# Soft-MoE attention on one core: five instead of four half batches of output stored between the last weight loads

## The chip, the core and the metric

The kernel runs on one core of a Trainium2 chip. The metric is the device time of one execution in microseconds (us). Data goes between device memory and the on-chip buffers by DMAs, which the queue of SyncE (SP) issues one after another and 16 DMA engines carry out. TensorE (PE) multiplies, VectorE (DVE) and ScalarE (ACT) copy and do elementwise work.

## The reference

An attention with a sigmoid in place of the softmax gives x, 3584 tokens by 768. A soft mixture of experts then mixes the tokens into 32 slots, sends each group of four slots through its own expert (two matrices), and mixes the slots back into tokens. Cut to what matters:

```python
scores = scale * np.matmul(q, k.transpose(0, 1, 3, 2)) - np.log(S)   # 8 batches, 12 heads, 448 tokens, 64
attn_out = np.matmul(1.0 / (1.0 + np.exp(-scores)), v)
x = attn_out.transpose(0, 2, 1, 3).reshape(B * S, H * D)             # 3584 x 768
logits = x @ phi                                                     # 32 slots, 4 for each of 8 experts
slot_input = softmax(logits, axis=0).T @ x
for e in range(E):                                                   # w1: 8 x 768 x 1024, w2: 8 x 1024 x 768
    slot_out[e] = np.maximum(slot_input[e] @ w1[e], 0.0) @ w2[e]
out = softmax(logits, axis=1) @ slot_out                             # 3584 x 768, float32
```

## The kernel before

The attention runs first, batch by batch, and takes some 280 us. What follows is the part that the change touches. The expert weights come in 128 units of 128 x 768 numbers (384 KB each): 64 of w1, then 32 of w2 for the first 384 output columns (`hf` 0), then 32 of w2 for the last 384 (`hf` 1). Each unit takes the next tile of a ring of 68 (`ring_tile`, `wa0` to `wa46` and `wb0` to `wb20`; L77). The first 68 units are loaded during and right after the attention. Of the rest, `load_more` (L509) puts one load behind a piece of work that has freed a tile, up to a limit of 128 - `N_LATE`: in the kernel before, units 0 to 111 are in SP's queue that way, and the last 16 are left over. I call these the late units; they are numbers 112 to 127.

The first product with w2 gives `st`, the slot outputs for columns 0 to 383. With it the first half of the output can be computed, while the second product with w2 still runs. That is the loop at L613, of 16 steps. Step i multiplies units 96 + 2i and 97 + 2i (`w2_step`, L588). In steps 3 to 10 it also computes the first column half of one batch's output, batch i - 3 (`out_batch`): eight matmul instructions (L565), an ACT copy of 128 rows and a DVE copy of 96 rows (L570) into two tiles of the same ring, and four stores that are put on a list. A half batch is 448 rows of 384 numbers: two stores of 192 KB and two of 144 KB, 672 KB together, each by its own DMA (L579).

Where those stores and the late loads stand in SP's queue is written out by hand: in the first `N_MIX` of these steps, `store(4)` issues the four stores of the half batch, and then `N_LATE // N_MIX` late units are loaded. The other half batches stay on the list until all loads are issued (L626). So SP's queue is, before: unit 111, four stores, four units, four stores, four units, four stores, four units, four stores, units 124 to 127, and then 16 stores in a row. Steps 10 to 13 have a few multiplications that compute nothing (`warm`, L583).

After the last `w2_step` comes a chain: ACT copies the sum (`gather`, L594), PE adds the groups (L599), DVE copies the result to `st` (L601), PE computes the second half of batch 0's output (L565), ACT and DVE copy it (L570), and SP stores it (L579). Then follow batches 1 to 7 in the same way, 32 stores in all.

SP takes its instructions in order, and each DMA also waits for one of eight completion counters that are used in turn: it can't be issued before the eighth DMA ahead of it has landed.

Of the kernel before, what the change touches and what calls it, by code (L numbers as in the profile page):

```python
# [26 lines left out]
UNIT = 768  # L27
N_A = 47
N_B = 21
N_LATE = 16  # L30
N_MIX = 4
NATT = 5
QW = 2 * S
NP = B * NPR
# [13 lines left out]
def soft_moe_attention(ctx: ExitStack, tc: tile.TileContext, qk, v, phi, w1, w2, cst, out):  # L48
# [36 lines left out]
    def load_unit():  # L85
        n = state["next"]
        if n >= len(units):
            return
        state["next"] = n + 1
        u = units[n]  # L90
        t = ring_tile()[:]
        nc.sync.dma_start(t, w1[u[1:]] if u[0] == "w1" else w2[u[1:]])
        utile[u] = t
# [415 lines left out]
    def load_more():  # L509
        if state["next"] < len(units) - N_LATE:  # L510
            load_unit()
# [49 lines left out]
    def out_batch(hf, b, st):  # L561
        pf = [px_tile() for _ in range(2)]
        for j in range(4):
            r = slice(32 * j, 32 * j + 32)
            nc.tensor.matmul(  # L565
                pf[j // 2][0:TOK[j], j % 2, 0:HALF], lt_all[r, b, 0:TOK[j]], st[r, :], start=True, stop=True)
        for g in range(2):
            n = TOK[2 * g]
            ov = ring_tile()[0:n, :].rearrange("p (j c) -> p j c", j=2)
            (nc.scalar.copy if g == 0 else nc.vector.tensor_copy)(ov, pf[g][0:n, :, 0:HALF])  # L570
            r0 = b * S + TOF[2 * g]
            for j in range(2):
                stores.append((out[r0 + j * n:r0 + j * n + n, hf * HALF:(hf + 1) * HALF], ov[:, j, :]))
# [3 lines left out]
    def store(n):  # L577
        for _ in range(min(n, len(stores))):
            nc.sync.dma_start(*stores.popleft())  # L579
# [33 lines left out]
    for i in range(2 * E):  # L613
# [3 lines left out]
        if 3 <= i < 3 + B:  # L617
            out_batch(0, i - 3, st)
            if i < 3 + N_MIX:
                store(4)  # L620
                for _ in range(N_LATE // N_MIX):
                    load_unit()
# [43 lines left out]
```

## Time and profile before

| | |
|---|---|
| time, median of 3 runs | 391.66 us (391.07 to 392.79) |
| profiled execution, its time | 390.38 us |
| its span, from the first to the last instruction | 388.6 us |
| PE busy | 365.3 us (94% of the span) |
| DVE busy | 226.1 us (58%) |
| ACT busy | 187.5 us (48%) |
| DMA, mean over the span | 251 GB/s |

The profiled execution took 390.38 us, 1.8 us more than its span. All stretches and durations below are of this one execution. PE's busy share is an average over stages: the attention is PE's, while the end of the program, from about 290 us, has to be read by itself, since there the DMA engines are always busy. Times of single instructions count from the start of the span. A DMA has three times that matter: when SP issues it, how long the issuing instruction holds SP, and how long after the issue the data has landed.

### The profile page before, as it was taken

To read this page: it belongs to the slowest core of one execution; us is meant where nothing else is said; L and a number is where in the kernel's file an instruction comes from. 1 tells how busy PE (TensorE), PEld (TensorE's weight loads), DVE (VectorE), ACT (ScalarE), POOL (GpSimd) and SP (SyncE) were. 2 spreads that over 40 slices of the span, in tenths; PEclk is the share of its full clock that TensorE was granted. 3 is DMA by queue.
4 is the path that set the end of the run, shared out by engine and by line. 5 is a ranking of instruction groups with operands and counts; after the bars stand their busy time and mean duration, and the time that the engine had idled before them with its cause. 6 is when DMAs were issued, how large, how long until landed. Compare 5 with 4: busy or idle time off the path is not lost.

```text
span 388.6 us, 9551 instructions
## 1 busy us (share of the span) xinstructions
PE 365.3 (94%) x3994; PEld 189.8 (49%) x3994; DVE 226.1 (58%) x518; ACT 187.5 (48%) x243; POOL 3.3 (1%) x13
## 2 busy tenths in 40 slices
PE   8999999999999999999999999999989989978760
PEld 7444556554555654555554455554455543224220
DVE  3655677775887677697767777776543410430250
ACT  5655676564567556566635666564531110320240
POOL 1000000000000000000000000000020000000000
PEclk9999999999999999999999999999999999999995
DMA  7766855662784567476446654323999999999997
GB/s 228 260 240 236 300 171 183 237 252 83 265 295 138 178 229 255 135 257 240 177 140 228 238 164 156 143 101 98 292 406 400 400 400 400 398 407 399 373 302 231
DMA packets 42363, 97.52 MB, mean 251 GB/s; under 512 B 4816, under 2 KB 16720, under 8 KB 42320
## 3 DMA queue, kind: packets, MB, share of 16 engines
q1 hardware_dynamic: 42320, 96.91, 70.3%
q8 instruction: 31, 0.51, 0.5%
q14 instruction: 12, 0.10, 0.1%
HBM read 85.43 MB, written 11.47 MB: 249 GB/s over the span
## 4 chain that ended last, share of the span: by engine, by line
PE 80%; DMA 14%; DVE 1%; SPq 1%; ACT 1%; issue 0%; ACTq 0%
PE b L189 29%; PE b L171 24%; DMA wa<-in_w_dram 8%; PE b L182 6%; DMA wb<-in_w_dram 6%; PE b L198 5%; PE b L312 4%; PE px L522 4%; PE b L218 3%; PE b L407 1%; PE px L565 1%; PE px L539 1%; SPq L579 1%; DMA out_dram<-wa 1%; DVE wa L570 0%
## 5 line engine op out<-in xcount | busy, mean ns | idle before, releaser
L161 ACT ACTIVATE att<-b,nbias 128x896 f32<-128x896 f32 x144 | 131.9, 1015 | 12.0 <-PE b L171 12.0
L189 PE MATMUL b<-att,v 128*64 128x448 f32 x576 | 115.3, 545 | 0.0
L171 PE MATMUL b<-qs,ks 64*128 64x448 f32 x864 | 95.9, 372 | 0.0
L171 PEld LDWEIGHTS b<-qs,ks 64*128 64x128 f32 x864 | 77.4, 184 | 26.6 <-PE b L182 11.3
L189 PEld LDWEIGHTS b<-att,v 128*64 128x64 f32 x576 | 38.5, 136 | 61.6 <-issue 50.2
L161 ACT ACTIVATE attm<-b,nbias 128x896 f32<-128x896 f32 x24 | 24.2, 1008 | 70.4 <-PE b L182 70.4
L207 DVE COPY xT<-b 128x896 f32<-128x896 f32 x23 | 25.1, 1092 | 32.7 <-PE b L198 32.7
L152 DVE TENSOR_TENSOR qs<-qkt,qs 128x448 fp32r<-128x448 f32 x48 | 30.0, 625 | 1.7
L152 DVE TENSOR_TENSOR ks<-qkt,ks 128x384 fp32r<-128x384 f32 x48 | 26.8, 558 | 1.6
L213 DVE STREAM_TRANSPOSE y<-xT 128x448 f32<-128x448 f32 x48 | 27.3, 617 | 0.4
L182 PE MATMUL b<-qkt 64*64 64x448 f32 x192 | 24.1, 570 | 0.0
L150 DVE CAST qs<-qkt 128x448 fp32r<-128x448 f32 x48 | 18.2, 380 | 8.8 <-DMA qkt<-in_qk_dram 7.7
L198 PE MATMUL b<-attm,v 64*64 64x448 f32 x192 | 22.4, 537 | 0.0
L570 DVE COPY wa<-px 96x768 f32<-96x768 f32 x13 | 12.2, 952 | 13.7 <-PE px L565 12.9
L570 ACT COPY wa<-px 128x768 f32<-128x768 f32 x13 | 10.3, 799 | 18.1 <-PE px L565 14.2
L565 PE MATMUL px<-st,lt_all 32*128 32x384 f32 (+1 forms) x128 | 16.7, 524 | 1.5 <-DVE st L601 0.7
L312 PE MATMUL b<-y,dr 32*32 32x192 f32 x896 | 17.7, 331 | 0.2 <-ACT dr L303 0.2
L218 PEld LDWEIGHTS b<-xT,phit 128*32 128x32 f32 x384 | 9.1, 109 | 17.0 <-issue 13.4
L522 PE MATMUL px<-wa,sT 128*32 128x256 f32 x282 | 16.8, 381 | 0.6 <-DVE sT L380 0.6
L150 DVE CAST ks<-qkt 128x384 fp32r<-128x384 f32 x47 | 16.6, 353 | 0.0
L218 PE MATMUL b<-xT,phit 128*32 128x96 f32 (+1 forms) x384 | 16.0, 266 | 0.2
L601 DVE COPY st<-px 128x384 f32<-128x384 f32 x2 | 1.1, 557 | 25.3 <-PE px L599 25.3
(132 smaller groups left out, 229.3 us busy)
## 6 DMA issues: line engine op xcount, KB each, us to landing
wa<-in_w_dram SPq DMA_DIRECT2D x92, 384.0 KB, 7.7
qkt<-in_qk_dram SPq DMA_DIRECT2D x48, 448.0 KB, 3.8
wb<-in_w_dram SPq DMA_DIRECT2D x36, 384.0 KB, 5.7
v<-in_v_dram SPq DMA_DIRECT2D x24, 448.0 KB, 5.7
out_dram<-wa SPq DMA_DIRECT2D x26, 192.0 KB, 3.3
out_dram<-wa SPq DMA_DIRECT2D x26, 144.0 KB, 3.3
dr<-zd SPq DMA_DIRECT2D x28, 64.0 KB, 2.0
out_dram<-wb SPq DMA_DIRECT2D x6, 192.0 KB, 5.5
```

The lines of the kernel that those rows point to most:

```text
L150: copy(dst[:, 0, :], src)
L152: nc.vector.tensor_tensor(out=dst[:, 1, :], in0=src, in1=dst[:, 0, :].bitcast(F32), op=ALU.subtract)
L161: nc.scalar.activation(att[:], sc[:, :, 0:S], AF.Sigmoid, bias=nbias, scale=QSCALE)
L171: nc.tensor.matmul(sc[:, h, 0:S], ks[r, z, c * P:(c + 1) * P], qs[r, y, :], start=(z + y == 0), stop=(z == 1))
L182: nc.tensor.matmul(sc[r, h, 0:S], t[d, S + NQK:QW], t[d, 0:S], start=True, stop=True)
L189: nc.tensor.matmul(avs["p", p][r, 0:S], vs[n][:, i * (NFULL + 1) + c, r], atts[p, c][:, h, :], start=(start and c == 0), stop=(stop and c ...
L198: nc.tensor.matmul(avs["p", 2 * n + i][d, 0:S], vt[r, NFULL, d], att[r, h, :], start=start, stop=stop)
L207: nc.vector.tensor_copy(xTs[n][:], avs[n][:, :, 0:S])
L213: nc.vector.transpose(ys[b][:, hp, :], xTs["p", p])
L218: nc.tensor.matmul(lp[32 * j:32 * j + 32, 0:TOK[j]], phi_sb[:, p % NPR, :], xTs["p", p][:, TOF[j]:TOF[j] + TOK[j]], start=(first and m == ...
L312: nc.tensor.matmul(sl[a // 2][32 * j:32 * j + 32, a % 2, 0:NPR * BLK], drs[b][32 * a:32 * a + 32, j, c * BLK:(c + 1) * BLK], y[32 * a:32 * ...
L522: nc.tensor.matmul(ph[32 * j:32 * j + 32, uu, 0:256], sT[:, 3 * kh + kc, :], utile[("w1", e, 2 * uu + j // 2, kh)][:, kc * 256:(kc + 1) * ...
```

## The change

Two constants change. `N_LATE` goes from 16 to 15, so unit 112 is loaded by `load_more`, ahead of the first stores. `N_MIX` goes from 4 to 5, so five half batches are stored among the late loads, each followed by 15 // 5 = 3 units instead of four. Nothing is added or removed: there are as many loads, stores, copies and matmuls as before, of the same sizes.

```diff
-N_LATE = 16
-N_MIX = 4
+N_LATE = 15
+N_MIX = 5
```

In SP's queue, at the first half batch that is stored (`wa_4226` and `wa_4228` are its two output tiles before, `wa_4228` and `wa_4230` now; `wa_4234` before and `wa_4029` now hold unit 112; - is before, + is now; "x2" is two instructions in a row):

```order
 L92 DMA wa_4019<-in_w_dram 128x768
-L579 DMA out_dram<-wa_4226 128x384 x2
-L579 DMA out_dram<-wa_4228 96x384 x2
-L92 DMA wa_4234<-in_w_dram 128x768
+L92 DMA wa_4029<-in_w_dram 128x768
+L579 DMA out_dram<-wa_4228 128x384 x2
+L579 DMA out_dram<-wa_4230 96x384 x2
 L92 DMA wb_4236<-in_w_dram 128x768
```

Unit 112 moved ahead of the four stores of batch 0's first half; unit 113 keeps its place.

In SP's queue, at the last loads, before (`wb_4312` to `wb_4318` are units 124 to 127, the stores behind them those of batches 4 and 5):

```order
L92 DMA wb_4312<-in_w_dram 128x768
L92 DMA wb_4314<-in_w_dram 128x768
L92 DMA wb_4316<-in_w_dram 128x768
L92 DMA wb_4318<-in_w_dram 128x768
L579 DMA out_dram<-wa_4330 128x384 x2
L579 DMA out_dram<-wa_4332 96x384 x2
L579 DMA out_dram<-wa_4344 128x384 x2
L579 DMA out_dram<-wa_4346 96x384 x2
```

and now (units 122 to 124, the stores of batch 4, units 125 to 127, the first stores of batch 5):

```order
L92 DMA wb_4308<-in_w_dram 128x768
L92 DMA wb_4310<-in_w_dram 128x768
L92 DMA wb_4312<-in_w_dram 128x768
L579 DMA out_dram<-wb_4324 128x384 x2
L579 DMA out_dram<-wb_4326 96x384 x2
L92 DMA wb_4332<-in_w_dram 128x768
L92 DMA wa_4334<-in_w_dram 128x768
L92 DMA wa_4336<-in_w_dram 128x768
L579 DMA out_dram<-wa_4348 128x384 x2
```

The four stores of batch 4's first half moved from behind unit 127 to ahead of unit 125. Twelve stores are left behind the last load, where 16 were.

On PE, at the last two steps of the second product with w2 (units 124 to 127; the order of PE's instructions is the same, only the tiles that the units lie in differ):

```order
 L583 MATMUL po<-csb 128x128 x3
 L588 MATMUL po<-wb_4312,h_3681 32x384 x2
-L588 MATMUL po<-wb_4314,h_3681 32x384 x2
-L588 MATMUL po<-wb_4316,h_3681 32x384 x2
-L588 MATMUL po<-wb_4318,h_3681 32x384 x2
+L588 MATMUL po<-wb_4332,h_3681 32x384 x2
+L588 MATMUL po<-wa_4334,h_3681 32x384 x2
+L588 MATMUL po<-wa_4336,h_3681 32x384 x2
```

Three of these four units now stand behind the fifth half batch's stores in the queue, where all four stood together.

## Rows read from the trace of the kernel before

**Rows 1.** The page's second part, the span in 40 equal slices of 9.7 us: the mean busy share of the DMA engines in tenths, and what they moved.

```profile
DMA  7766855662784567476446654323999999999997
GB/s 228 260 240 236 300 171 183 237 252 83 265 295 138 178 229 255 135 257 240 177 140 228 238 164 156 143 101 98 292 406 400 400 400 400 398 407 399 373 302 231
```

**Rows 2.** The chain of work that ended last, in order of time, from 339.67 us: start, duration, what it was. A DMA's duration here is from its issue to its landing.

```profile
339.67 5.40 DMA wb<-in_w_dram
...
345.13 5.40 DMA wb<-in_w_dram
...
350.60 5.46 DMA wb<-in_w_dram
...
356.12 6.00 DMA wb<-in_w_dram
...
362.17 0.86 PE po L588 x4
...
363.11 0.49 ACT tmp L594
...
363.64 0.93 PE px L599 x2
...
364.59 0.57 DVE st L601
...
365.20 0.94 PE px L565 x6
...
366.16 0.81 ACT wa L570
...
366.99 0.54 SPq L579
```

**Rows 3.** Busy time of the engines in two stretches, from the first store to the first store of the second column half, and from there to 387.5 us. The last three columns are PE's granted clock, the DMA engines' busy share and GB/s.

```profile
334.00:366.97 32.97, 27.04 (x188) 9.09 (x182) 8.57 (x10) 7.25 (x11) 0.00 (x0) 1.00 1.04 398
366.97:387.50 20.53, 7.78 (x52) 3.04 (x52) 6.70 (x8) 5.48 (x7) 0.00 (x0) 0.76 0.88 288
```

**Rows 4.** SP's queue in order of time: start, time until the last of the group had been issued, line, what, how many. Groups of four unit loads and of four stores between the first late loads and the last.

```profile
342.26 3.20 SPq L92 DMA_DIRECT2D wb<-in_w_dram  x4
345.64 1.91 SPq L579 DMA_DIRECT2D out_dram<-wb  x4
347.76 3.16 SPq L92 DMA_DIRECT2D wb<-in_w_dram  x4
351.21 1.88 SPq L579 DMA_DIRECT2D out_dram<-wb  x4
353.27 3.17 SPq L92 DMA_DIRECT2D wb<-in_w_dram  x4
```

**Rows 5.** The same view, three unit loads in a row ahead of the first store, and the first store.

```profile
329.92 0.33 SPq L92 DMA_DIRECT2D wa<-in_w_dram  x1
330.89 0.33 SPq L92 DMA_DIRECT2D wa<-in_w_dram  x1
331.87 0.33 SPq L92 DMA_DIRECT2D wa<-in_w_dram  x1
334.40 0.34 SPq L579 DMA_DIRECT2D out_dram<-wa  x1
```

**Rows 6.** ACT in order of time: the copies of batch 4's and batch 7's first half (idle time before them in brackets, with what ended it).

```profile
341.38 0.80 ACT L570 COPY wa<-px 128x768 f32<-128x768 f32 x1 [1.11 <-PE px L565]
...
350.42 0.80 ACT L570 COPY wa<-px 128x768 f32<-128x768 f32 x1 [2.78 <-DMA out_dram<-wb]
```

**Rows 7.** The stores' line in the stretch 362.5 to 366.5 us, after the last load has landed: how many, duration of the issuing instruction (least, median, most, ns), first and last start; and from issue to landing. Then the first and the last of these eight issues in SP's order of time.

```profile
L579 SPq DMA_DIRECT2D out_dram<-wa x8: 351/425/450, 362.7 to 366.1; - x8
...
DMA to landing us min/median/max: 3.1/3.3/3.6
...
362.68 0.35 SPq L579 DMA_DIRECT2D out_dram<-wa  x1
...
366.07 0.44 SPq L579 DMA_DIRECT2D out_dram<-wa  x1
```

**Rows 8.** The same line from 366.9 to 385 us, the 32 stores of the second column half, with the last issue.

```profile
L579 SPq DMA_DIRECT2D out_dram<-wa x32: 350/442/727, 367.0 to 384.2; - x32
...
DMA to landing us min/median/max: 2.8/3.3/3.7
...
384.25 0.50 SPq L579 DMA_DIRECT2D out_dram<-wa  x1
```

**Rows 9.** What SP waited for from 366.9 us to the end (us in total, times, longest); L662 is the end of the program.

```profile
SPq L662 <- DMA out_dram<-wa: 2.8, 2, 2.4
SPq L579 <- ACT wa L570: 0.6, 2, 0.4
SPq L662 <- PEq L662: 0.6, 2, 0.4
SPq L579 <- DVE wa L570: 0.2, 1, 0.2
```

**Rows 10.** PE in order of time, at the last steps of the second product with w2 and in the output of the second half (idle time before the group in brackets).

```profile
359.26 2.75 PE L588 MATMUL po<-wb,h 128*32 128x384 f32 x12 [1.46 <-DMA wb<-in_w_dram]
362.17 0.84 PE L588 MATMUL po<-wb,h 128*32 128x384 f32 x4 [0.16 <-DMA wb<-in_w_dram]
...
368.96 3.56 PE L565 MATMUL px<-st,lt_all 32*128 32x384 f32 x24 [0.35 <-DVE wa L570]
372.71 2.70 PE L565 MATMUL px<-st,lt_all 32*128 32x384 f32 x16 [0.19 <-DVE wa L570]
```

**Rows 11.** Stretches after PE's last matmul; the third number from the right is the granted clock.

```profile
376.50:377.00 0.50, 0.00 (x0) 0.00 (x0) 0.00 (x0) 0.00 (x0) 0.00 (x0) 1.00 1.00 313
...
378.00:379.00 1.00, 0.00 (x0) 0.00 (x0) 0.00 (x0) 0.00 (x0) 0.00 (x0) 0.50 0.95 298
```

## The prediction

> **What bounds the kernel now.** I read the slices first. In the last quarter of the span the DMA engines' share is 9 in every slice, at about 400 GB/s, and in the last three slices it stays high while the rate falls to 302 and 231 [rows 1]. So the end belongs to DMA in some form, and the question is which form where. The chain answers that [rows 2]. Up to 362.12 us it is a row of unit loads, each issued when an earlier one has landed: PE waits for weights, weights wait for their place in a full queue. The last load is issued at 356.12 and lands 6.00 us later. Then comes a chain that moves almost nothing: the last four matmuls (0.86), `gather` (0.49), the sum over groups (0.93), the copy to `st` (0.57), batch 0's second half on PE (0.94), its ACT copy (0.81), and at 366.99 the first store of the second half. From there on 32 stores are left.
>
> Two stretches, then. Up to 366.97 the engines move 398 GB/s at a share of 1.04; behind it 288 GB/s at 0.88 [rows 3]. In the second stretch, who is the limit? SP issues 32 stores between 366.99 and 384.25, so one every 17.26 / 31 = 0.557 us; the issuing instruction alone holds it for 0.442 (median), and a store lands 3.3 us after its issue, as it did at 363 to 366 us [rows 2, 7, 8]. SP waits for a copy for only 0.6 + 0.2 us in all of that, and for no earlier store's landing [rows 9]. If the engines were the limit and SP ran ahead, eight DMAs would be under way and a landing would take 8 x 0.557 = 4.5 us. It takes 3.3, with no growth. I therefore read the last stretch as SP's: it starts when the first second-half copy is ready, and its length is 32 issues plus one landing.
>
> **The change part by part.** *The batch that moves ahead of the last load.* Up to the last load the DMA engines are full, so what is put in front of it delays it. Unit 112 only changes places with a group of stores and stays ahead of the last load in both; the one thing that crosses is four stores, 672 KB. Its cost there, three ways:
>
> - From the cycle: groups of four loads start at 342.26, 347.76 and 353.27, so a cycle of four loads and four stores is 5.50 us [rows 4]. Loads alone go one per (331.87 - 329.92) / 2 = 0.975 us [rows 5]. The stores' part is 5.50 - 3.90 = 1.60.
> - From the bytes: 672 KB are 0.688 MB, at 398 GB/s [rows 3] 1.73 us.
> - From stores with no loads beside them: eight issues from 362.68 to 366.07, so 0.484 us each [rows 7], four are 1.94.
>
> I take 1.7, nearest to the first two, since those rows are of the mixed stretch into which the batch goes; the ends are 1.6 and 1.94.
>
> *Does SP wait for the moved batch's copies, with three loads behind it?* The copies of batch 4's first half start at 341.38 and take 0.80 (ACT) [rows 6]. Now its stores come to their turn after three cycles of 5.50 and three of three loads each; counted from the first store at 334.40 [rows 5], four cycles of 3 x 0.975 + 1.7 = 4.6 give about 353. That wait costs nothing, and there are 11 us of cover.
>
> *The twelve stores left behind the last load.* Before, SP finished issuing the sixteenth at 366.07 + 0.44 = 366.51 and stood until the copy was ready at 366.97 [rows 2, 7]. So these stores already fit into the time of the chain, with 0.46 us to spare. Four fewer of them give SP a longer pause, 4 x 0.484 = 1.9 us more, in which nothing else is ready. This is where the expected gain would have to be, and it is spent on waiting: the work that was taken out had cover, and the place it was put into has none.
>
> *The chain from the last landing to the first second-half store* keeps its instructions, 366.99 - 362.12 = 4.87 us, and begins 1.7 later. PE's last steps meet their units one by one as before; the longest wait there is 1.46 us [rows 10]. Units 125 to 127 come 1.7 later than before, 124 at the same time, so the added wait falls between 124 and 125 and does not stack on the old one in full.
>
> *The last 32 stores.* Same number, same issuing engine. Bounds: 0 if the pace stays 0.557; up to 4 x (0.557 - 0.484) = 0.3 us more, if the first few went at the quicker pace of the stretch before, which now has ended earlier [rows 7, 8]. I take 0.
>
> Sum: 390.38 + 1.7 = 392.1 for the profiled execution. It lies 1.28 below the median of the runs shown, so on the median 391.66 + 1.7 = **393.4 us**, 0.43% slower. From the bounds, +1.6 to +2.24: 393.3 to 393.9.
>
> **The rivals.** *B, the last stretch is the DMA engines' own.* Then they finish all weights and first-half stores at the same moment as before, a later first copy is absorbed, and the moved batch costs less in the mixture than at the end: 4 x 0.557 = 2.23 there [rows 8], 1.7 here, so -0.5, at most -0.63: 391.0 to 391.2 us, *faster*. For it: a share of 0.88 and more is not idle [rows 3], and the issuing instruction sometimes lasts 0.727 [rows 8], as if it were held. Against it: landings of 3.3 us and SP's 0.46 us pause with nothing to store.
> The Trainium skill has a rule on this side: the page "DMA: Bandwidth & Descriptors", section "Issuing engines are not separate DMA queues", says that the time a sequencer needs to start a DMA is usually small beside the DMA itself. By that rule the last stretch would be the engines' and the time rival B's. The trace speaks against it for stores of this size: 0.442 us of holding SP in every 0.557.
>
> *C, PE's clock falls while it waits for the late units.* The granted clock is 1.00 in the whole first stretch, waits of 1.46 us included [rows 3, 10], but after PE's last matmul it is still 1.00 at 376.5 and 0.50, the lower level of 1.2 GHz, from 378 [rows 11]. It decides if PE's waits before units 125 to 127, which grow by about 1.7 us between them, run together into one that is clearly longer than 1.46. The matmuls of the chain (0.86 + 0.93 + 0.94 = 2.73 [rows 2]) would then take twice that: +1.7 + 2.7, so 396.1 us, clearly slower. If the low clock went on, a batch of eight matmul instructions, (2.70 / 2 = 1.35 [rows 10] and its waits), would be near SP's 4 x 0.557 and cost more still. Against it: warm-up matmuls fill part of the wait, and the waits are cut up by the arrival of each unit.
>
> *D, the moved batch rides for free*, writes beside reads: 391.7 us. The cycle speaks against it, since stores already cost 1.60 of 5.50 there [rows 4].
>
> **How the numbers follow.** The forecast 0.74, B 0.15, C 0.06, D 0.05. About 0.5% (2.0 us) is what a measurement of this kernel can tell from no change. The forecast's band lies on both sides of +2.0, more of it below: 0.27 above, 0.47 within. C is above, B and D within, but for 0.03 for B with more gain than I can work out. So faster 0.03, same 0.64, slower 0.33. The range goes from B's far end, 391.66 - 0.63 = 391.0, to 393.9 and half a us for the spread of the runs, 394.4; C and a little of the rest lie outside. The forecast's own range is 393.0 to 394.4.
>
> **What would show it.** Right: in the chain the last load lands near 363.8 instead of 362.12 and the first second-half store is issued near 368.7; SP then stands for about 2 us for an ACT copy ahead of it; 32 stores follow at 0.55 to 0.56 us each, landing in about 3.3; the last is issued near 386. Wrong: if the last load lands as late as I say but the last store does not move (then B), if the 32 stores come closer together than 0.5 us (B too), if the last load lands within 0.5 us of before (D), or if the granted clock drops below 1.00 ahead of 370 us (C).

## The result, and the profile after

The changed kernel takes 395.18 us (median of 22 executions), the kernel before 392.53 (22, beside them). The ratio is 1.007, with a 95% interval of 1.0053 to 1.0087: **2.7 us slower (2.1 to 3.4)**. Forecast were 1.7. The direction and the path were right; the size was not, and the time lies above the range, which ended at 394.4. Two things add up there. The forecast of 393.4 stood on three executions of the kernel before with a median of 391.66; the 22 beside the changed kernel have 392.53. Of the 1.8 us between 393.4 and 395.18, 0.87 is that base and 0.95 is the change itself. Counted from its own base, the slowdown of 2.65 would have lain just inside the range (394.4 - 391.66 = 2.74).

The profiled execution has a span of 392.2 us, 3.6 more than the one before. The chain of work that ended last, in order of time (start, duration, what; a DMA from issue to landing), as in [rows 2]:

```profile
333.59 7.86 DMA wa<-in_w_dram
...
341.51 5.36 DMA wb<-in_w_dram
...
346.93 5.40 DMA out_dram<-wb
...
352.35 5.18 DMA out_dram<-wb
...
357.59 0.33 SPq L579
...
357.98 0.70 SPq L579
...
358.77 1.26 SPq L92
...
360.13 0.45 SPq L92
...
360.67 5.67 DMA wa<-in_w_dram
...
366.38 0.86 PE po L588 x4
...
367.32 0.49 ACT tmp L594
...
370.38 0.81 ACT wa L570
```

The first row is unit 111, the last load ahead of everything that the change moves. It was issued at 331.87 before [rows 5] and at 333.59 here, 1.72 later: that much of the 3.6 comes from the attention ahead, differs from execution to execution, and has nothing to do with the change. So I count from unit 111. The `gather` copy then starts 363.11 - 331.87 = 31.24 us later before and 367.32 - 333.59 = **33.73** here: 2.5 us more, where the sum said 1.7. The chain behind is the same as before. One thing in it was not on the path before: ahead of the last load SP itself stands there, with store and load issues of 0.33, 0.70, 1.26 and 0.45 us one behind the other. A long hold alone is not new, though. The kernel before has one too, at unit 124, beside its path:

```profile
353.27 1.23 SPq L92 DMA_DIRECT2D wb<-in_w_dram  x1
```

SP's queue in the changed kernel, in order of time (start, time until the last of the group had been issued):

```profile
344.35 1.97 SPq L92 DMA_DIRECT2D wb<-in_w_dram  x3
346.93 1.87 SPq L579 DMA_DIRECT2D out_dram<-wb  x4
348.89 2.18 SPq L92 DMA_DIRECT2D wb<-in_w_dram  x3
351.52 2.47 SPq L579 DMA_DIRECT2D out_dram<-wb  x4
354.08 1.64 SPq L92 DMA_DIRECT2D wb<-in_w_dram  x3
356.33 2.35 SPq L579 DMA_DIRECT2D out_dram<-wb  x4
358.77 1.26 SPq L92 DMA_DIRECT2D wb<-in_w_dram  x1
```

Three cycles take 358.77 - 344.35 = 14.42 us, 4.81 each. A cycle of four loads took 5.50 [rows 4]; with one load less, 0.975 [rows 5], it should be 4.53. Each is 0.28 dearer than that.

Stretches around the end of the chain (the last three columns are granted clock, DMA share and GB/s):

```profile
366.00:368.00 2.00, 1.26 (x7) 0.29 (x6) 0.00 (x0) 0.48 (x1) 0.00 (x0) 1.00 1.04 378
368.00:370.00 2.00, 1.35 (x10) 0.60 (x12) 0.56 (x1) 0.00 (x0) 0.00 (x0) 1.00 1.01 348
370.00:372.00 2.00, 1.75 (x20) 0.82 (x14) 0.95 (x1) 1.50 (x2) 0.00 (x0) 1.00 0.38 136
372.00:374.00 2.00, 1.65 (x18) 0.51 (x12) 1.82 (x2) 0.80 (x1) 0.00 (x0) 1.00 0.94 318
```

In 370 to 372 the engines move 136 GB/s: the twelve stores are done, the chain is not. That is the gap where the moved batch used to be. The last 32 stores and what SP waits for from the first of them on, as in [rows 8, 9]:

```profile
L579 SPq DMA_DIRECT2D out_dram<-wa x32: 351/432/1307, 371.2 to 388.7; - x32
...
DMA to landing us min/median/max: 1.9/2.9/3.6
...
SPq L579 <- ACT wa L570: 2.6, 2, 1.8
```

They take from 371.2 to 388.7, (17.5 / 31 = 0.56 us each), as before. Ahead of the first, SP stood 1.8 us for ACT's copy.

### The profile page after: what moved, and what is told of

Same layout as the page of the kernel before. It is cut to its first block, busy times and chain, and to the rows that moved or that the text cites. A ratio compares the mean times of both kernels' runs of the same rounds, so it can differ in the third digit from the quotient of the medians.

```text
span 392.2 us, 9551 instructions
## 1 busy us (share of the span) xinstructions
PE 368.0 (94%) x3994; PEld 190.6 (49%) x3994; DVE 225.9 (58%) x518; ACT 187.5 (48%) x243; POOL 3.3 (1%) x13
## 4 chain that ended last, share of the span: by engine, by line
PE 80%; DMA 13%; DVE 1%; SPq 1%; ACT 1%; issue 0%; ACTq 0%
PE b L189 29%; PE b L171 24%; DMA wa<-in_w_dram 9%; PE b L182 6%; PE b L198 5%; PE b L312 4%; PE px L522 4%; PE b L218 3%; DMA out_dram<-wb 3%; PE px L565 2%; DMA wb<-in_w_dram 1%; PE b L407 1%; DVE wa L570 1%; PE px L539 1%; SPq L92 0%
## 5 line engine op out<-in xcount | busy, mean ns | idle before, releaser
L198 PE MATMUL b<-attm,v 64*64 64x448 f32 x192 | 23.4, 538 | 0.1
L570 DVE COPY wa<-px 96x768 f32<-96x768 f32 x12 | 11.3, 952 | 12.8 <-PE px L565 9.2
L570 ACT COPY wa<-px 128x768 f32<-128x768 f32 x12 | 9.5, 799 | 17.0 <-PE px L565 13.2
```

The costliest lines, as they stand in the source:

```text
L198: nc.tensor.matmul(avs["p", 2 * n + i][d, 0:S], vt[r, NFULL, d], att[r, h, :], start=start, stop=stop)
```

## The experiments

Times are ratios to the kernel before in executions beside them, with the 95% interval, and in us. A second measure comes from the profiles, which is freer of the attention's scatter: from the issue of unit 111 to the start of the `gather` copy. Beside it stand the time from the same issue to the landing of the last load, which leaves PE's last step out, and what the DMA engines moved in that time. All of it in one table; the sections refer to it.

| kernel | unit 111 | `gather` | between | last load | GB/s | ratio | against before, us |
|---|---|---|---|---|---|---|---|
| before | 331.87 | 363.11 | 31.24 | 30.25 | 401 |  |  |
| before, second profile | 333.12 | 364.68 | 31.56 | 30.58 | 399 |  |  |
| chain delay (same up to there) | 333.64 | 365.81 | 32.17 | 31.18 | 378 | 1.0047 (1.0025 to 1.0068) | +1.8 |
| changed | 333.59 | 367.32 | 33.73 | 32.75 | 389 | 1.007 (1.0053 to 1.0087) | +2.7 |
| changed, second profile | 333.37 | 368.81 | 35.44 | 33.80 | 369 |  |  |
| changed, two queues | 331.80 | 366.52 | 34.72 | 33.08 | 391 | 1.0062 (1.0042 to 1.0082) | +2.4 |
| changed, more warm-up | 333.29 | 367.62 | 34.33 | 33.34 | 382 | 1.0044 (1.0014 to 1.0074) | +1.7 |
| changed, merged at the end | 333.15 | 368.03 | 34.88 | 33.90 | 375 | 1.0059 (1.003 to 1.0087) | +2.3 |
| changed, merged among loads | 333.55 | 366.19 | 32.64 | 31.66 | 405 | 1.0003 (0.9975 to 1.0031) | +0.1 |
| changed, merged in both | 333.29 | 365.63 | 32.34 | 31.36 | 405 | 1.0023 (1.0004 to 1.0043) | +0.9 |
| before, merged among loads | 333.18 | 364.05 | 30.87 | 29.88 | 401 | 0.9963 (0.994 to 0.9987) | -1.5 |
| before, merged in both | 332.41 | 363.13 | 30.72 | 29.74 | 405 | 0.9997 (0.9968 to 1.0027) | -0.1 |
| four half batches, three loads each | 332.88 | 365.26 | 32.38 | 31.39 | 386 | 0.9997 (0.9977 to 1.0018) | -0.1 |

**Is it the number of half batches or the number of loads between them?** Five half batches with four loads each:

```diff
-N_LATE = 16
-N_MIX = 4
+N_LATE = 20
+N_MIX = 5
```

> N_LATE 20 and N_MIX 5: five half batches among the loads, as in the changed kernel, but four loads behind each, as in the kernel before. Theory 'bytes' (a half batch ahead of the last load costs its 0.688 MB at the engines' rate, whatever the grouping): the last load lands as late as in the changed kernel, the time is about 2.7 us above the kernel before. Rival 'grouping' (three loads to four stores make each cycle dearer; four to four don't): a cycle is 5.5 us again, the one half batch costs 1.6, the time is 1.6 us above the kernel before.

Measured: 1.0141 (1.0116 to 1.0166), 5.5 us slower. Neither theory had that. The stretches show why: here SP reaches the first half batch's stores with only unit 107 issued, and stands until they are computed, while all loads queue behind.

```profile
334.00:337.00 3.00, 2.87 (x22) 0.73 (x20) 0.44 (x1) 0.50 (x1) 0.00 (x0) 1.00 0.90 350
337.00:340.00 3.00, 3.00 (x30) 0.89 (x24) 1.47 (x2) 1.10 (x2) 0.00 (x0) 1.00 0.39 139
340.00:342.00 2.00, 0.30 (x4) 0.00 (x0) 0.95 (x1) 0.80 (x1) 0.00 (x0) 1.00 0.95 274
342.00:346.00 4.00, 1.62 (x8) 0.38 (x8) 0.00 (x0) 0.00 (x0) 0.00 (x0) 0.79 0.96 269
```

The engines ran dry at 337 to 340 (139 GB/s), a stall that neither kernel has. The run tells nothing on the question; it shows what it costs to put a store ahead of its time.

Four half batches, three loads each:

```diff
-N_LATE = 16
+N_LATE = 12
```

> N_LATE 12 and N_MIX 4: as many half batches ahead of the last load as before, but three loads behind each. 'Bytes': nothing crosses the last load, no change, within 0.5 us. 'Grouping': each of four cycles costs 0.3 us more (4.82 us seen in the changed kernel against 4.52 = 5.50 - 0.975), the time is 1.2 us above the kernel before.

Measured: 0.9997 (0.9977 to 1.0018), no change, as "bytes" had it; 1.2 us lies outside the interval. In its profile the cycles are dear as well ((356.31 - 341.67) / 3 = 4.88 us) and the between time is 32.38, 0.7 above the mean of the three profiles with the kernel before's mixture (31.66) and 0.2 above the highest of them. Its rate is low as well, 386 GB/s. So a cost of 0.7 is possible at the edge of the interval, but four dearer groups by themselves are not shown to cost time.

**A second profile of each.**

> The changed kernel once more, for a second profile. In the first, the last load landed 32.75 us after the issue of unit 111, where it was 30.25 in the kernel before. If the dearer mixture belongs to the change, this stretch is again 32 us or more and the cycles 4.7 us or more; if it was an accident of one execution, it is 31.9 (30.25 + 1.6) or less.

The last load landed after 33.80 us, more and not less, and two cycles (344.12 to 353.51 us) took 4.70 each. So the dearer mixture belongs to the change. In this execution one store's issue held SP for 2.65 us, in this group of SP's queue of the second profile (4.05 us for four stores, where 1.9 is usual):

```profile
356.74 4.05 SPq L579 DMA_DIRECT2D out_dram<-wb  x4
```

And the clock fell. PE in order of time, with its idle time in brackets:

```profile
365.04 1.01 PE L588 MATMUL po<-wb,h 128*32 128x384 f32 x4 [1.76 <-DMA wb<-in_w_dram]
366.09 2.62 PE L588 MATMUL po<-wa,h 128*32 128x384 f32 x8
```

and two stretches of the same profile, granted clock third from the right:

```profile
364.00:366.00 2.00, 0.96 (x4) 0.14 (x4) 0.00 (x0) 0.00 (x0) 0.00 (x0) 0.89 0.81 283
366.00:368.00 2.00, 1.95 (x10) 0.37 (x8) 0.00 (x0) 0.00 (x0) 0.00 (x0) 0.50 1.04 386
```

PE's last step took 2.62 us at a granted clock of 0.50 (1.2 GHz) instead of 1.78 in the first profile: rival C, in some executions. It adds 0.7 us between the last landing and `gather` (1.64, where the first profile has 0.98).

> The kernel before once more, for a second profile. If the first profile of it was a typical one, the last load again lands 30.2 to 30.5 us after the issue of unit 111 and the granted clock is 1.00 until the second half's output is computed; if its mixed stretch can lose time as well (the chain-delay kernel, with the same mixture, needed 31.2), 31 us or more.

The last load after 30.58 us, 31.56 between, the clock at 1.00 to the end of PE's work: near the first. The chain delay's 31.18, with the same mixture, shows that the kernel before can lose time there too.

**Does the clock make part of the loss?** The changed kernel with more warm-up:

```diff
         if 2 + B <= i < 2 * E - 2:
-            warm(3)
+            warm(3 if i == 2 + B else 6)
```

> The changed kernel with six warm-up matmuls instead of three in steps 11 to 13, so that PE is busy for most of its wait for the late units. In the changed kernel 12 of 22 executions have a mean clock of 0.984 or less, 10 of 52 in the kernel before. If the clock that falls while PE waits makes part of the loss: nearly all executions at 0.985 or more, and 0.5 us faster than the changed kernel (2.2 us above the kernel before instead of 2.7). If it plays no part: the same clocks or the same time.

The clocks came out as said: none of 12 executions at 0.984 or less, against 12 of 22 of the changed kernel and 24 of the 110 of the kernel before that ran in these comparisons. The time is 1.0044 (1.0014 to 1.0074). It is lower than 1.007, but the intervals overlap: that the clock falls more often is shown, that it costs 1 us is not. The changed kernel's own 22 executions say no more: the 12 with the lower clock have a mean of 395.64 us, the other ten 394.94. That is 0.7 us apart, within their scatter, and the ten are still 2.3 above the kernel before (mean 392.61). Three profiles with the clock at 1.00 up to the end of PE's work are dear all the same (33.73, 34.33 and 34.88 between). So the clock is not the main part of the loss.

**Do the small stores make the mixture dear?** One store for each output tile instead of two, so that a half batch is two DMAs and not four:

```diff
-            for j in range(2):
-                stores.append((out[r0 + j * n:r0 + j * n + n, hf * HALF:(hf + 1) * HALF], ov[:, j, :]))
+            stores.append((
+                out[r0:r0 + 2 * n, hf * HALF:(hf + 1) * HALF].rearrange("(j p) c -> p j c", j=2), ov))
...
-                store(4)
+                store(2)
...                                             # the same in the last loop
```

In both halves, on the kernel before and on the changed one:

> The kernel before with one store for each output tile instead of two (256 or 192 rows of 1536 B in one DMA; 16 in the last stretch instead of 32, and two instead of four between the loads). If an issue has a fixed cost on SP that sets the pace of the last stretch: the stretch gets 2 to 3 us shorter, 389.5 to 390.5. If the cost is by rows, or the pace is the engines': no change in the last stretch, within 0.5 us. In the mixed stretch twice the bytes are under way with eight DMAs; if that was short of bytes before, the last load lands earlier too.

> The changed kernel with one store for each output tile instead of two, so that a half batch takes two of the eight DMAs that can be under way, not four. If the changed kernel's dearer cycle (4.82 us for three loads and a half batch, where 3 x 0.975 + 1.6 = 4.5 would do) comes from too few bytes under way: cycles of 4.5 us, the last load lands 1.6 to 1.7 us later than in the kernel before with merged stores, the time is 393.5. If it comes from the finer mixture of reads and writes: cycles stay at 4.8, the time is 394.5.

0.9997 (0.9968 to 1.0027) and 1.0023 (1.0004 to 1.0043). Between: 30.72 and 32.34, a difference of **1.62**, the forecast's price of a half batch. (In time these two differ by 1.0 us, with an uncertainty of about 1.4, an estimate from the two intervals.) But merging might help at the end of the program too, so three more runs take it apart, with the edit above under `if hf == 0` (the first column half, among the loads) or `if hf == 1` (the second, at the end):

> The changed kernel with merged stores for the first column half alone, so the last 32 stores are as in the changed kernel. From the issue of unit 111 to the copy of the second product's sum it took 33.7 and 35.4 us in the two profiles of the changed kernel, 31.2 and 31.6 in those of the kernel before, 32.3 with merged stores in both halves. If the loss beyond 1.7 us lies in the mixture of many small DMAs with loads: 32.3 us here, and 1.6 us slower than the kernel before. If merged stores only help the last stretch: 33.7 us or more, and 2.7 us slower.

> The changed kernel with merged stores for the second column half alone. If the loss beyond 1.7 us lies in the mixture: 33.7 us or more from unit 111 to the copy of the sum, and still 2.7 us slower than the kernel before, less what merging gives the last stretch. If merging helps in the last stretch alone: 0.9 us slower, as with merged stores in both halves.

> The kernel before with merged stores for the first column half alone: the base of the first of these three. 30.7 us from unit 111 to the copy of the sum, as with merged stores in both halves, so 1.6 us less than in the first; the time within 0.5 us of the kernel before, or up to 0.7 us faster.

The third, the kernel before with merged stores among the loads, is 0.9963 (0.994 to 0.9987), 1.5 us faster than the kernel before: of all kernels run, the one that beats both. Its profile shows less of a gain, 0.4 to 0.7 between against the two profiles of the kernel before, and with merged stores in both halves no gain was measured; so the size of it is uncertain. The first is at 1.0003, so the moved half batch costs 0.1 + 1.5 = 1.6 us with merged stores (again give or take 1.4). The second is at 1.0059, still 2.3 slower. So it is the mixture, and not the end. SP's queue in the first, as above:

```profile
342.51 2.00 SPq L92 DMA_DIRECT2D wb<-in_w_dram  x3
345.12 1.28 SPq L583 DMA_DIRECT2D out_dram<-wb  x2
347.03 1.97 SPq L92 DMA_DIRECT2D wb<-in_w_dram  x3
349.65 1.28 SPq L583 DMA_DIRECT2D out_dram<-wb  x2
351.53 2.03 SPq L92 DMA_DIRECT2D wb<-in_w_dram  x3
```

Cycles of 347.03 - 342.51 = 4.52 and 351.53 - 347.03 = 4.50: just one load less than 5.50, with the same bytes as in the changed kernel, whose cycles are 4.81.

The engines' rate says the same. From unit 111's issue to the last landing, in the kernel before, the changed kernel, the changed and the kernel before with merged stores among the loads (GB/s is the last number):

```profile
331.87:362.12 30.25, 25.86 (x184) 8.67 (x184) 7.63 (x8) 6.39 (x8) 0.00 (x0) 1.00 1.04 401
333.59:366.34 32.75, 26.97 (x184) 8.80 (x184) 7.63 (x8) 6.38 (x8) 0.00 (x0) 1.00 1.04 389
333.55:365.21 31.66, 26.77 (x186) 8.81 (x184) 7.63 (x8) 6.39 (x8) 0.00 (x0) 1.00 1.04 405
333.18:363.06 29.88, 25.86 (x184) 8.68 (x184) 7.63 (x8) 6.38 (x8) 0.00 (x0) 1.00 1.04 401
```

The changed kernel's mixture of small stores moves 369 to 391 GB/s in its five profiles; with merged stores, four profiles have 401 to 405; the kernel before has 399 and 401, and 378 once, in the chain delay's profile. So what the sum left out is not more bytes but a lower rate of the engines.

Long holds of SP are not enough to explain it. The kernel before with merged stores among the loads has them as well, up to 1.42 us (SP's load issues from 337 us to the last one; the three durations are the least, the median and the most, in ns):

```profile
L92 SPq DMA_DIRECT2D wb<-in_w_dram x15: 339/447/1422, 337.3 to 355.7; - x15
```

Its rate is 401 GB/s all the same. There a load lands some 7.3 us after its issue, where it is 5.4 with small stores [rows 2], so more work is under way while SP is held.

**What sets the pace of the last 32 stores?** Half of them from ACT's queue:

```diff
         out_batch(1, b, st)
-        store(4)
+        for _ in range(2):
+            nc.scalar.dma_start(*stores.popleft())
+        store(2)
```

> The changed kernel with half of the last 32 stores (those of ACT's copies) issued from ACT's queue. If SP's issuing sets the pace of the last stretch: a store every 0.43 to 0.46 us (0.172 MB at 398 to 380 GB/s) instead of 0.557, 31 x 0.1 = 3 us less than the changed kernel, so about the time of the kernel before or just below. If the DMA engines set it: the pace stays at 0.55 us and the time that of the changed kernel, 2.7 us above the kernel before.

1.0062: no gain over the changed kernel. In its profile, though, the granted clock is 0.50 from 364 us to the end, so PE set the pace there; the run doesn't decide. The kernel with merged stores at the end does. The 16 stores' row and their landing:

```profile
L583 SPq DMA_DIRECT2D out_dram<-wa x16: 400/902/1289, 371.9 to 386.4; - x16
...
DMA to landing us min/median/max: 2.8/4.5/5.0
```

Half as many issues, and each holds SP for 0.902 instead of 0.432 us (in the median; the least, 0.400, is that of the first). The landings have grown to 4.5: SP now runs ahead, and the engines are the limit. From the first of these stores to the end it is 391.8 - 371.9 = 19.9 us, against 392.2 - 371.2 = 21.0 in the changed kernel. Over all profiles that stretch takes 20.3 to 21.6 us with small stores from one queue and 19.9, 20.6 and 21.4 with merged ones. Halving SP's issues bought 1 us at the most.

**Does the chain start the last stretch?** The kernel before with the `gather` copy made four times:

```diff
-    def gather(po):
+    def gather(po, n=1):
...
-        nc.scalar.copy(so[:], po[:, 0:HALF])
+        for _ in range(n):
+            nc.scalar.copy(so[:], po[:, 0:HALF])
...
-    so = gather(po)                             # of the second product
+    so = gather(po, 4)
```

> The kernel before with the copy of the second product's sum made four times instead of once (the same numbers again), so that the chain behind the last load is 3 x 0.49 = 1.5 us longer and nothing else moves. If the last stretch starts with the first copy of the second half and has a length of its own (the prediction's reading): 1.5 us slower. If the DMA engines' work sets the end and the sixteen stores left over cover the wait: no change, at most 0.3 us.

1.0047 (1.0025 to 1.0068), 1.8 us slower (1.0 to 2.7). But more than the copies moved. PE stood 2.16 us for them, and the granted clock was 0.50 from 368.8 to 375.6 us, in the output of the second half:

```profile
367.87 0.91 PE L600 MATMUL px<-tmp,csb 128*128 128x384 f32 x2 [2.16 <-ACT tmp L595]
369.00:370.00 1.00, 0.57 (x4) 0.50 (x8) 0.38 (x1) 0.00 (x0) 0.00 (x0) 0.50 1.01 338
```

The first store of the second half is issued 371.95 - 333.64 = 38.3 us after unit 111, where it was 35.1 and 35.4 in the two profiles of the kernel before. Of these 3 us, 1.5 are the copies, 0.7 the first batch at the low clock (1.70 us from its first matmul to ACT's copy instead of 0.96), and the rest is the mixed stretch. From that store to the end it is 20.3 us, where it was 21.6 and 21.2. So a later chain does move the end, and some 1 us of it is absorbed. How much of the 1.5 us alone would reach the end is not settled: 11 of the 12 executions have a mean clock of 0.984 or less, and the twelfth took 392.69 us, no more than the kernel before (392.80).

**And the other way: fewer half batches ahead of the last load.** Three, with five loads each (small stores); then, with merged stores in both halves, two with eight, and none:

```diff
-N_LATE = 16
-N_MIX = 4
+N_LATE = 15
+N_MIX = 3
```

> N_LATE 15 and N_MIX 3: one half batch less ahead of the last load than in the kernel before, twenty stores behind it. The last load lands 1.6 us earlier; by the prediction's reading SP has issued the twenty stores about 366.85 (366.51 - 1.6 + 4 x 0.484), so the first store of the second half comes at the same moment as before: no change, within 0.5 us. If each half batch ahead of the last load cost its 1.7 us whatever is left behind it: 1.7 us faster.

```diff
-N_MIX = 4
+N_MIX = 2
```

> Merged stores with only two half batches among the loads and eight loads behind each (N_MIX 2). Each half batch behind the last load instead of ahead of it brings the last load forward by 1.62 us, 3.2 us for two, and with merged stores SP had 3.7 us to spare ahead of the first second-half store. If the chain sets the start of the last stretch: 2 to 3.2 us faster than merged stores with four, 389.5. If what is moved behind comes back as engine time in the last stretch: 0 to 1 us faster.

```diff
-N_LATE = 16
-N_MIX = 4
+N_LATE = 0
+N_MIX = 0
...
-                for _ in range(N_LATE // N_MIX):
+                for _ in range(0):
```

> Merged stores with no half batch among the loads: all 128 units ahead of all stores. The last load lands 4 x 1.62 = 6.5 us earlier than in the kernel before. Left over are 32 merged stores, 11 MB: at 398 GB/s throughout 27.7 us behind the last landing, which gives 388 to 388.5 us; if the last 5.5 MB go at the 330 GB/s of the merged last stretch, 390. If the end hangs on the chain alone: 386.

1.0021 (0.9998 to 1.0045), 1.0025 (1.0001 to 1.0048) and 1.0041 (1.001 to 1.0071): no change or slower, up to 1.6 us; for the last two, no theory had forecast a loss. In the first, SP did not stand for the chain at all: twenty stores just fill its wait. The last is the plainest. Its `gather` starts at 358.22, 24.4 us after unit 111's issue at 333.83 and so 7 us earlier than before, and the time is worse. Its last load lands at 357.23. The stretches around and behind that:

```profile
356.00:358.00 2.00, 1.81 (x10) 0.29 (x8) 0.00 (x0) 0.00 (x0) 0.00 (x0) 1.00 1.06 399
358.00:360.00 2.00, 1.03 (x4) 0.30 (x2) 0.30 (x1) 0.48 (x1) 0.00 (x0) 1.00 1.07 396
360.00:364.00 4.00, 3.15 (x24) 1.44 (x24) 2.15 (x4) 2.20 (x3) 0.00 (x0) 1.00 0.95 319
364.00:368.00 4.00, 3.70 (x28) 1.57 (x32) 3.01 (x5) 2.50 (x4) 0.00 (x0) 1.00 0.94 293
368.00:372.00 4.00, 2.49 (x16) 0.70 (x16) 2.54 (x3) 1.60 (x2) 0.00 (x0) 1.00 0.90 277
```

With 32 stores in a row ready for SP, the engines move stores alone at 396 GB/s for some 3 us and then at 319, 293 and 277. Why they begin at the rate of the loads and then fall is not shown. Merged stores beside loads cost 1.6 us for a half batch; in a long row by themselves, at 290 GB/s, it is 0.688 / 0.290 = 2.4, an estimate.

## Why the prediction was wrong

- **The DMA engines bound the mixed stretch, and the chain runs from the last load through the gather to the first second-half store**: right, but the engines did not keep their 398 GB/s, and in the changed kernel SP's own issues stand on the path for 3 us ahead of the last load.
- **The moved batch costs 1.7 us**: this is the term that was mis-sized. With merged stores it is right: between times of 32.49 (mean of 32.64 and 32.34) against 30.80 (30.87 and 30.72), 1.69 us, and 1.0 to 1.6 us of time. With the kernel's small stores the five profiles have a mean of 34.62 against 31.66 for three of the kernel before, 2.96; to the last landing, without the low clock of PE's last step in two of them, it is 33.37 against 30.67, 2.70; and the time is 2.7. The step took the stores' part, 1.60, from the cycle of four loads and the 398 GB/s from the mixture of four, and assumed, without saying so, that the *other four* half batches keep their price when each is followed by three loads. They did not: cycles of 4.81 where 4.53 was due, at 389 GB/s instead of 401. Those rows were not to be had before, but the doubt was: the change alters every group, and I costed only the one that crosses. The rest of the distance from 393.4 to 395.18 is the base, 0.87, which three executions gave too low.
- **The sixteen stores already fit into the chain's time, so taking four away only makes a pause**: right. SP stood 1.8 us for ACT's copy, 2.5 in the second profile; 1.9 + 0.46 were worked out.
- **The last stretch is SP's**: wrong as a cause. The engines, once a row of stores alone has lasted some us, do 277 to 332 GB/s (none among the loads, merged at the end); SP's issues and the engines were near balance, which is why landings of 3.3 us looked like an idle queue. What was drawn from it, that the stretch begins with the chain and has a length of its own, held for the most part: it takes 21.2 to 21.6 us where SP stood at most 0.5 us ahead of it, and 20.3 to 21.0 where it stood 1.9 or more, so that 0.6 us of a later start is absorbed in the mean. Rival B had the right limit and the wrong result: the engines had run out of stores (136 GB/s) before the chain was done, so little was left to absorb a later start. That the forecast came out right in direction with the wrong engine as the limit is in part luck.
- **Rival C**, given 0.06: it did not replace the forecast, but it comes on top in part of the executions (12 of 22 at a mean clock of 0.984 or less, which took 0.7 us longer than the others). Its share in time is small and not settled.
- **Rival D**: refuted; the batch does not ride for free (2.7 us with small stores, 1.0 to 1.6 with merged ones).

What stays open is why the mixture with small stores is dear. It goes away when a half batch is two DMAs instead of four, with the same rows and bytes. Of the eight DMAs that may be under way, more are then loads, and SP has fewer issues; these two were not told apart, though long holds of SP did no harm where the DMAs under way were large. Nor is it settled why four groups of three loads lost no measurable time and five did.

## What to carry to other kernels

A change to an interleaving re-prices every group of it, not only the piece that crosses the boundary: cost the new ratio, or bound it by the worst cycle in sight. Work that fills the wait of a chain is free where it stands, and moving it ahead of what the chain waits for costs nearly its full price. Where DMAs in flight are limited by number, try large ones before arranging them: merging each pair of stores among the loads gave 1.5 us (0.5 to 2.4) in the kernel before and 2.6 in the changed one, and no count of half batches gave anything.

## What the runs showed of the hardware that was not expected

- The engines' rate depends on what they carry, in what pieces and for how long: from unit 111 to the last landing 401 to 405 GB/s with merged stores among the loads, 399 and 401 (378 once) with four small stores to four loads, 369 to 391 with four small stores to three loads. Stores of 1536-byte rows alone went at 396 for some 3 us (none among the loads) and then at 277 to 319, with stores always waiting in SP's queue and from one issuer.
- An issuing instruction on SP can be held far beyond its usual 0.33 to 0.45 us: 1.26 and 2.65 us in the two profiles of the changed kernel, 1.23 in the kernel before, 1.42 with merged stores, all in the mixed stretch. Behind the 2.65 the engines fell to 265 GB/s (362 to 364 us).
- PE's clock fell to 0.50 in one profile of the changed kernel after a wait of 1.76 us between matmuls, where a wait of 1.46 in the kernel before had left it at 1.00 [rows 10, 11]. The length of one wait does not tell, though. In the second profile of the kernel before, the clock stayed at 1.00 after 1.60 us; with two queues it fell at 363.6 us, in a wait of 0.87 us that came 0.84 us of work after one of 1.46 (the first row is the former, the other two the latter):

```profile
360.89 3.69 PE L588 MATMUL po<-wb,h 128*32 128x384 f32 x16 [1.60 <-DMA wb<-in_w_dram]
...
362.27 0.84 PE L588 MATMUL po<-wb,h 128*32 128x384 f32 x4 [1.46 <-DMA wb<-in_w_dram]
363.98 2.44 PE L588 MATMUL po<-wa,h 128*32 128x384 f32 x8 [0.87 <-DMA wa<-in_w_dram]
```
